# A fused attention and two-layer-stack kernel on one core: weight preparation timed by its own load, a swapped load buffer, a later restart of the conversion, one second product moved

## The chip, the cores and the metric

The kernel runs on one core of a Trainium2 chip. The metric is the device time of one execution in microseconds (us). "PE" is TensorE, "DVE" VectorE, "ACT" ScalarE, "POOL" GpSimd and "SP" SyncE, which here only issues DMAs.

## The reference, cut to what matters

```python
x = attention(q, k, v, mem_k, mem_v)          # windows of 32 queries, 56 keys with 8 memory keys; [1536, 512]
p = probs / (probs.sum(-1) + 1e-9)
y = sum(p[:, e] * (relu(x @ w1[e]) @ w2[e]) for e in range(4))     # w1[e]: 512 x 1024, w2[e]: 1024 x 512
h = y @ w_in                                   # 512 x 2048
out = (relu(h) + alpha * minimum(h, 0)) @ w_out                    # 2048 x 512
```

Everything is float32, but `w_in` and `w_out` reach the chip as 64-bit words and are turned into float32 there.

## The kernel before, in words

**The tiles.** After the attention the work is a row of 24 *pairs* of 128 hidden features: pairs 0 to 15 belong to the four experts, pairs 16 to 23 to the last layer. The two halves of the 1536 tokens are worked together, so a tile is a pair times 384 columns, and each pair has two tiles (columns 0 and 384). For a tile k there are two pieces of PE work. `gemm1` (line 565), the first product, is a Strassen-like scheme of seven products named by their banks in the order a, b, d, a, c, d, c, of 6 matmuls each, 42 in all. `gemm2` (line 652), the second product, has 8 blocks of 6 matmuls, all called `y`, 48 in all. Every matmul is 128x128 by 128x384. The 6 come from float32 split into a high and a low half: high by high, high by low, low by high.

**What the other engines do for a tile.** In `gemm1` ACT copies the first bank (`u`), DVE adds the banks (`u`, `t`, `b`, `d`, `c`), and bank a, d and c are each written a second time, which waits until those reads are done. `gelu` (line 593) makes the activation `g`: for the experts one DVE operation, for the last layer two on ACT and one on DVE. ACT casts it to the high half (`gg`) and POOL subtracts to get the low half. In `gemm2` each of the 8 blocks is added to `acc` by DVE (copied by ACT for pair 0, by DVE for pair 16).

**Order of the PE's work.** `order` (lines 758 to 769) is written out. It starts first product of tile 0, second of 0, first of 1, second of 1, then first of 2, first of 3, second of 2, and so on with the second product one tile behind. Pairs 14 and 15, and 16 and 17, are interleaved column by column (tiles 28 to 35); there two first products are followed by one double second product (`gemm2_two`, line 707, 96 matmuls). `acc` is the output of the experts there, and `transition` (line 183) turns it, one half of the columns at a time, into the next layer's input `xh`/`xl` with ACT, DVE and POOL, while tiles 30 and 31, then 32 and 33, are computed.

**The planner.** Each engine runs its program in the order in which it was written out. That order is made by a planner with a clock `now[0]`, which goes on by 0.013 + 384/2400 = 0.173 us with each matmul. Before each matmul it writes out whatever other work is due. There are two streams: "w" prepares the weights, "c" converts.

**Weights ("w", lines 375 to 468).** Each pair has a first matrix (z = 0) and a second (z = 1), 512 KB each. `load_raw` issues its DMA from SP into a buffer called raw0 or raw1, one of each. `prep_w1` makes four sums (`s`), then casts (ACT, `wh`) and subtracts (`wl`) seven pieces; `prep_w2` casts and subtracts two pieces of double size. Sums and subtractions are on POOL, for the pairs in `QUICK` = (1, 15, 17) on DVE at shorter steps (`DT_FAST` 0.45 instead of 1.1). At its end `prep_w1(p)` loads the next pair's first matrix, and `prep_w2(p)` the next second one. `WIDE` = (15, 17) are the pairs which need four extra pieces in tiles shared with the conversion (tags `ft`, `fr`), free only while `change[0]` is set and no conversion chunk is under way (`room_w1`). `weights` (line 460) gives the order: before a wide pair, its `prep_w1` comes ahead of the `prep_w2` of the pair before it. So `prep_w1(15)` and `prep_w1(17)` begin the moment after they issued their own loads.

**Conversion ("c", lines 473 to 514).** 32 chunks, four to a pair of the last layer, each a load (`fr`), five DVE operations (`fm`, `fw`), one on ACT, two on POOL (`fl`), and a store to `w2s` in DRAM, from where `load_raw` reads pairs 16 to 23. The planner starts one each 15 us (`T_CONV`), the DVE part 6 us behind the load. The first comes 20 us after tile 2's first product begins. None starts while `change[0]` is set, which is so from the first product of tile 27 to the beginning of that of tile 35.

Of the kernel before, what the change touches and what calls it, by code (L numbers as in the profile page):

```python
# [10 lines left out]
F32 = mybir.dt.float32  # L11
# [20 lines left out]
P = 128  # L32
# [4 lines left out]
NCOL = NT // 2  # L37
NP1 = E * F1 // (2 * P)
NP2 = F2 // (2 * P)
NP = NP1 + NP2  # L40
# [25 lines left out]
def tile_kernel(ctx: ExitStack, tc: tile.TileContext, qk, v, wa, wq, dpt, alpha, out):  # L66
# [6 lines left out]
    bp = ctx.enter_context(tc.tile_pool(name="bp", bufs=1))  # L73
# [29 lines left out]
    now = [0.0]  # L103
# [38 lines left out]
    change = [False]  # L142
# [226 lines left out]
                x[0] = now[0]  # L369

    w2s = dp.tile([NP2, P, 2048], F32, name="w2s")
    raws, w1, w2 = {}, {}, {}
    used1, used2 = set(), set()

    def load_raw(p, z):
        raw = bp.tile([P, 4, 256], F32, tag=f"raw{z}", name=f"raw{z}_{p}")
        src = wa[p] if p < NP1 else w2s[p - NP1]
        sync.dma_start(raw.rearrange("p a f -> p (a f)"), src[:, z * 1024:(z + 1) * 1024])
        raws[p, z] = raw

    ring1 = []

# [13 lines left out]
        ring1.append((p, j))  # L396
        return tuple(bp.tile([P, 256], F32R, tag=f"w1{x}", bufs=SLOTS, name=f"w{x}1_{p}_{j}") for x in "hl")

    def pace(p):
        fast = p in QUICK  # L400
        return dve if fast else pool, DT_FAST if fast else DT if p else DT_0

    loaded = [0.0]

    def pause(t, cond=None):
        return now[0] + t, cond

    def prep_w1(p):

        e, dt = pace(p)  # L410
        yield pause(0.0, lambda: (p, 0) in raws)
        raw = raws[p, 0]
        a11, a12, a22, a21 = (raw[:, i] for i in range(4))
        s = bp.tile([P, 4, 256], F32, tag="S", name=f"s_{p}")
        src = {A11: a11, A12: a12, A22: a22, S1: s[:, 0], S2: s[:, 1], S3: s[:, 2], S4: s[:, 3]}
        for zo, x, y, op in (
            (S1, a21, a22, ALU.add), (S2, s[:, 0], a11, ALU.subtract),
            (S3, a11, a21, ALU.subtract), (S4, a12, s[:, 1], ALU.subtract),
        ):
            e.tensor_tensor(out=src[zo], in0=x, in1=y, op=op)  # L420
            yield pause(dt)
        for j, z in enumerate(USE):
            yield pause(0.0, lambda: room_w1(p, j))
            h, l = place_w1(p, j)
            act.copy(h, src[z])
            yield pause(dt)
            e.tensor_tensor(out=l, in0=src[z], in1=h.bitcast(F32), op=ALU.subtract)
            w1[p, z] = (h, l)
            yield pause(dt)
        raws.pop((p, 0))  # L430
        if p + 1 < NP:
            yield pause(0.0, lambda: conv_done(p + 1))
            load_raw(p + 1, 0)
            loaded[0] = now[0]

    def prep_w2(p):

        e, dt = pace(p)
        yield pause(0.0, lambda: p < 2 or p - 2 in used2)
        if p == 1:  # L440
            yield pause(0.0, lambda: att["done"] == 2 * NU)
        if p == 0:
            yield pause(0.0, lambda: (0, 1) in raws and began)
        raw = raws.pop((p, 1))
        h = bp.tile([P, 4, 256], F32R, tag="w2", bufs=4, name=f"wh2_{p}")
        l = bp.tile([P, 4, 256], F32R, tag="w2", bufs=4, name=f"wl2_{p}")
        for z in (0, 2):
            act.copy(h[:, z:z + 2], raw[:, z:z + 2])
            yield pause(1.5 * dt)
            e.tensor_tensor(  # L450
                out=l[:, z:z + 2], in0=raw[:, z:z + 2], in1=h[:, z:z + 2].bitcast(F32), op=ALU.subtract
            )
            if z == 2:
                w2[p] = (h, l)
            yield pause(1.5 * dt)
        if p + 1 < NP:
            load_raw(p + 1, 1)
            yield pause(max(0.0, loaded[0] + 6.0 - now[0]))

    def weights():  # L460
        for p in range(NP):
            if p not in WIDE:
                yield from prep_w1(p)
            if p + 1 in WIDE:
                yield from prep_w1(p + 1)
            yield from prep_w2(p)

# [184 lines left out]
    def gemm2(p, c0, n, gs, soon, last):  # L652
        prep_force("w", lambda: p in w2)
        wh, wl = w2[p]
        y = {}

        def part(o, ab, i, start, stop, z0=0, z1=n):
            lag_poll(lambda: 2 * i + ab in gs)
            gh, gl = gs[2 * i + ab]
            if start:  # L660
                y[o, ab] = bank(f"y{p}_{c0}_{o}_{ab}_{z0}")[:, :n]
            w_ = [x[:, 2 * i + o // 2, (o % 2) * P:(o % 2 + 1) * P] for x in (wh, wl)]
            for k, (a, b) in enumerate(((w_[0], gh), (w_[1], gh), (w_[0], gl))):
                product(y[o, ab][:, z0:z1], a, b[:, z0:z1], n=z1 - z0,
                        start=start and k == 0, stop=stop and k == 2)
            if stop:
                evac(p, c0 + z0, z1 - z0, o, ab, y[o, ab][:, z0:z1])

        if p == 0:

            for o in range(2):
                part(o, 0, 0, True, False)
            for o in range(4):
                part(o, 1, 1, True, False)
                part(o, 1, 0, False, True)
            for o in range(2):
                part(o, 0, 1, False, True)
            for o in range(2, 4):
                part(o, 0, 0, True, False)
                part(o, 0, 1, False, True)  # L680
        elif soon:

            for o in range(4):
                part(o, 0, 0, True, False)
            for o in range(2):
                part(o, 1, 1, True, False)
            for o in range(4):
                part(o, 0, 1, False, True)
            for o in range(2):
                part(o, 1, 0, False, True)  # L690
        else:
            for o in range(4):
                part(o, 0, 0, True, False)
                part(o, 0, 1, False, True)
            for o in range(2):
                part(o, 1, 1, True, False)
                part(o, 1, 0, False, True)
        for o in range(2, 4) if p else ():

            end = p == NP - 1 and c0 + n == NCOL and o == 3  # L700
            for z0, z1 in ((0, n // 2), (n // 2, n)) if end else ((0, n),):
                part(o, 1, 1, True, False, z0, z1)
                part(o, 1, 0, False, True, z0, z1)
        if last:
            used2.add(p)
# [49 lines left out]
    k0 = len(FIRST)  # L755
    kc = tiles.index((NP1 - 2, 0, half))
    order = []
    for k in range(k0):
        order += [(1, k), (2, k)]
    order += [(1, k0)]  # L760
    for k in range(k0 + 1, kc + 1):
        order += [(1, k), (2, k - 1)]
    order += [(1, kc + 1), (2, kc, kc + 1)]
    for k in range(kc + 2, kc + 8, 2):
# [21 lines left out]
    for i, (what, k, *other) in enumerate(order):  # L786
        p, c0, n = tiles[k]
        if k == k0 and what == 1:
            dve.tensor_scalar_mul(nalpha, nalpha, -1.0)
        if what == 1:  # L790
            if p == 0:
                while att["done"] < 4 * -(-(c0 + n) // BLK):
                    if k == 0:
                        att_cycle()
                    else:
                        att_poll(force=True)
                    prep_poll()
                    while begun and att["next"] >= begun[0][0]:
                        begun.pop(0)[1]()
                    if att["done"] >= 3 and not gated:  # L800
                        gated.append(gate())
                        begun.append((11, lambda: load_pb(0, *FIRST[0])))
                        begun.append((12, lambda: load_raw(0, 1)))
            if k == k0 - 1:
                attention_over()
            if k == k0:
                stream("c", convert())
                streams["c"][0] = now[0] + 20.0
            if k + 1 < len(tiles):
                p1, d0, m = tiles[k + 1]  # L810
                if p1 < NP1 and (2 * p1 * P // F1, d0, m) not in pb_t:
                    load_pb(2 * p1 * P // F1, d0, m)
            if p >= NP1 and f"x{c0}" in streams:
                prep_force(f"x{c0}", lambda: f"x{c0}" not in streams)
            began.append(k)
            change[0] = kc - 1 <= k < kc + 7
            acts[k] = gemm1(p, c0, n, k % 2 if p else 0, k == final[p])
        else:
            if other:
                gemm2_two(p, c0, n, [acts.pop(k), acts.pop(k + 1)], k == final[p])  # L820
            else:
                gemm2(p, c0, n, acts.pop(k), order[i - 1] == (1, k), k == final[p])
            if p == NP1 - 2:
                stream(f"x{c0}", transition(c0, n))
# [19 lines left out]
DT_FAST = 0.45  # L844
DT_CONV = 1.2
T_CONV = 15.0
DT_X = 1.1
RING = 4
RINGV = 3
# [75 lines left out]
```

## Time and profile before

| | |
|---|---|
| median of 3 runs | 852.46 us (851.75 to 853.57) |
| the profiled execution | 852.93 us, span 851.2 us |
| PE busy | 824.9 us of the span, 97% |
| DVE, ACT, POOL busy | 583.2, 336.9, 552.9 us |
| mean granted clock of PE | 0.99 of full speed |

Times in the rows below are from the start of the span. The profiled execution is 0.47 us above the median. A row of the timeline gives start, duration, engine, line and operation, with its output and inputs; in brackets stands how long the engine sat idle before it and what ended that.

### The profile page before, as it was taken

Reading aid. Unit: us, or ns where it says so; the run is one execution under the profiler, and the core shown is the slowest. Engines: PE = TensorE matmul, PEld = TensorE weight load, DVE = VectorE, ACT = ScalarE, POOL = GpSimd, SP = SyncE. Lnnn points to the kernel's source line nnn. Section 1 sums busy time; section 2 is a strip of 40 time slices with the busy share of each in tenths; the row PEclk is TensorE's granted clock in tenths of the full one; section 3 lists DMA queues with packets and bytes.
Section 4 is the critical chain, followed back from the end, with each engine's and each line's share of the span. In section 5 each row is a group of like instructions: output and inputs, shape, how many; then the busy total and the mean of one; then the engine's idle time right before and its main releaser. Section 6 shows DMA issues by size and latency. Waiting matters only on the chain.

```text
span 851.2 us, 15052 instructions
## 1 busy us (share of the span) xinstructions
PE 824.9 (97%) x5659; PEld 799.2 (94%) x5659; DVE 583.2 (69%) x1157; ACT 336.9 (40%) x754; POOL 552.9 (65%) x584
## 2 busy tenths in 40 slices
PE   8888999999999999999999999998898999999998
PEld 6656999999999999999999999998897999999998
DVE  4768656876777777776877857368844767666555
ACT  2555642232332332322322332145652746546432
POOL 3548466777877877867877944283743887876611
PEclk9999999999999999999999999999998999999999
DMA  8784202323312332322332212001002222221003
GB/s 234 191 245 140 75 10 78 97 89 100 112 52 86 124 105 80 99 85 77 106 106 75 87 38 75 1 26 50 25 17 71 87 79 89 82 75 50 1 1 148
DMA packets 30600, 71.70 MB, mean 84 GB/s; under 512 B 4800, under 2 KB 11072, under 8 KB 30528
## 3 DMA queue, kind: packets, MB, share of 16 engines
q1 hardware_dynamic: 30528, 70.75, 26.2%
q8 instruction: 44, 0.72, 0.4%
q14 instruction: 28, 0.23, 0.1%
HBM read 59.18 MB, written 11.56 MB: 83 GB/s over the span
## 4 chain that ended last, share of the span: by engine, by line
PE 83%; DVE 5%; POOL 4%; DMA 4%; issue 2%; ACT 2%; SPq 1%; DVEq 0%; POOLq 0%; ACTq 0%
PE y L60 43%; PE a L60 10%; PE c L60 10%; PE d L60 10%; PE b L60 5%; POOL gg L60 2%; POOL xl L60 1%; DMA v<-in_v 1%; POOL wl L60 1%; PE keep L60 1%; PE x L60 1%; DVE acc L60 1%; DVE s L60 1%; DMA raw<-w2s 1%; PE two L60 1%
## 5 line engine op out<-in xcount | busy, mean ns | idle before, releaser
L60 PE MATMUL y<-gg,wh 128*128 128x384 f32 x1540 | 403.6, 339 | 4.1 <-POOL gg L60 2.2
L60 PEld LDWEIGHTS y<-gg,wh 128*128 128x128 f32 x1540 | 280.4, 189 | 6.7 <-POOL gg L60 4.1
L60 POOL TENSOR_TENSOR gg<-g,gg 128x384 fp32r<-128x384 f32 x192 | 199.9, 1051 | 126.0 <-ACT gg L60 100.4
L60 PE MATMUL y<-gg,wl 128*128 128x384 f32 (+1 forms) x770 | 260.0, 338 | 0.0
L60 DVE TENSOR_TENSOR acc<-y,acc 128x384 f32<-128x384 f32 x321 | 171.4, 551 | 63.3 <-PE y L60 62.1
L60 ACT CAST gg<-g 128x384 fp32r<-128x384 f32 x192 | 97.5, 512 | 169.0 <-DVE g L60 168.9
L60 POOL TENSOR_TENSOR wl<-raw,wh 128x256 fp32r<-128x256 f32 (+1 forms) x105 | 105.2, 1014 | 77.3 <-ACT wh L60 49.3
L60 PEld LDWEIGHTS y<-gg,wl 128*128 128x128 f32 x770 | 145.4, 189 | 0.0
L60 ACT COPY u<-a 128x384 f32<-128x384 f32 x48 | 23.0, 479 | 179.5 <-PE a L60 179.5
L60 POOL TENSOR_TENSOR wl<-s,wh 128x256 fp32r<-128x256 f32 x84 | 65.3, 786 | 8.2 <-ACT wh L60 6.6
L60 PE MATMUL a<-xh,wh 128*128 128x384 f32 x184 | 62.7, 341 | 2.6 <-ACT u L60 2.6
L60 ACT CAST wh<-raw 128x256 fp32r<-128x256 f32 (+1 forms) x116 | 55.0, 493 | 24.9 <-DMA raw<-in_wa 11.9
L60 DVE TENSOR_TENSOR u<-b,u 128x384 f32<-128x384 f32 x48 | 26.7, 556 | 54.1 <-PE b L60 45.6
L60 PE MATMUL d<-xh,wh 128*128 128x384 f32 x184 | 62.5, 340 | 1.0 <-DVE t L60 1.0
L60 PE MATMUL a<-xl,wh 128*128 128x384 f32 x184 | 62.3, 339 | 0.0
L60 PE MATMUL a<-xh,wl 128*128 128x384 f32 x184 | 62.3, 338 | 0.0
L60 PE MATMUL d<-xl,wh 128*128 128x384 f32 x184 | 62.0, 337 | 0.0
L60 PE MATMUL d<-xh,wl 128*128 128x384 f32 x184 | 62.0, 337 | 0.0
L60 PE MATMUL c<-xh,wh 128*128 128x384 f32 x176 | 60.0, 341 | 0.0
L60 PE MATMUL c<-xh,wl 128*128 128x384 f32 x176 | 59.9, 341 | 0.0
L60 PE MATMUL c<-xl,wh 128*128 128x384 f32 x176 | 59.6, 339 | 0.0
L60 POOL TENSOR_TENSOR fl<-fl,fm 128x512 f32<-128x512 f32 x32 | 41.5, 1296 | 25.5 <-DVE fm L60 11.4
(113 smaller groups left out, 1398.6 us busy)
## 6 DMA issues: line engine op xcount, KB each, us to landing
raw<-in_wa SPq DMA_DIRECT2D x32, 512.0 KB, 3.7
fr<-in_wq SPq DMA_DIRECT2D x32, 512.0 KB, 3.9
w2s<-fl SPq DMA_DIRECT2D x32, 256.0 KB, 2.4
raw<-w2s SPq DMA_DIRECT2D x16, 512.0 KB, 3.6
qk<-in_qk SPq DMA_DIRECT2D x24, 312.0 KB, 4.8
v<-in_v SPq DMA_DIRECT2D x32, 130.0 KB, 4.5
pb<-p_dram SPq DMA_DIRECT2D x8, 384.0 KB, 3.5
outT<-acc SPq DMA_DIRECT2D x15, 192.0 KB, 1.9
```

The costliest lines, as they stand in the source:

```text
L60: return self.tc.keep_in_program_order(f(*a, **kw))
```

## The change: what it does

- The second product of tile 1 (pair 0, columns 384) moves behind the first product of tile 2. Its blocks run in the usual order, and its activations use the other set of buffers.
- `prep_w1` and `prep_w2` (but for the first pairs) wait until the planner's clock is 7 us (9 us for pairs 15 and 17) past the issue of their load; the pause of 6 us behind a load goes.
- `prep_w1(15)` comes behind `prep_w2(14)` instead of ahead of it. `prep_w1(17)` still comes ahead of `prep_w2(16)`.
- `prep_w2(16)` subtracts on DVE instead of POOL.
- Pair 17's second matrix is loaded into raw0, as soon as `prep_w1(17)` is through with it; pair 18's first matrix goes into raw1 after `prep_w2(16)`. From there on the two buffers have changed places.
- `change[0]` is set until tile 35's first product is over: the conversion resumes one first product later.

```diff
-    raws, w1, w2 = {}, {}, {}
+    raws, landed, w1, w2 = {}, {}, {}, {}
...
-        raw = bp.tile([P, 4, 256], F32, tag=f"raw{z}", name=f"raw{z}_{p}")
+        raw = bp.tile([P, 4, 256], F32, tag=f"raw{z if p + z < NP1 + 2 else 1 - z}", name=f"raw{z}_{p}")
...
+        landed[p, z] = now[0] + T_LOAD[p in WIDE]
...
-    def pace(p):
-        fast = p in QUICK
+    def pace(fast, p):
...
-        e, dt = pace(p)
-        yield pause(0.0, lambda: (p, 0) in raws)
+        e, dt = pace(p in QUICK, p)
+        yield pause(0.0, lambda: (p, 0) in raws and (p == 0 or landed[p, 0] <= now[0]))
...
-        if p + 1 < NP:
+        if p == NP1 + 1:
+            load_raw(p, 1)
+        elif p + 1 < NP:
             yield pause(0.0, lambda: conv_done(p + 1))
             load_raw(p + 1, 0)
-            loaded[0] = now[0]
...
-        e, dt = pace(p)
+        e, dt = pace(p in QUICK or p == NP1, p)
         yield pause(0.0, lambda: p < 2 or p - 2 in used2)
+        if p > 1:
+            yield pause(max(0.0, landed[p, 1] - now[0]))
...
-        if p + 1 < NP:
+        if p == NP1:
+            load_raw(p + 2, 0)
+        elif p + 1 < NP:
             load_raw(p + 1, 1)
-            yield pause(max(0.0, loaded[0] + 6.0 - now[0]))
...
-            if p not in WIDE:
+            if p != NP1 + 1:
                 yield from prep_w1(p)
-            if p + 1 in WIDE:
+            if p == NP1:
                 yield from prep_w1(p + 1)
...
-        if p == 0:
+        tight = p == 0 and c0 + n < NCOL
+        if tight:
...
-        for o in range(2, 4) if p else ():
+        for o in () if tight else range(2, 4):
...
-    for k in range(k0):
+    for k in range(k0 - 1):
         order += [(1, k), (2, k)]
-    order += [(1, k0)]
-    for k in range(k0 + 1, kc + 1):
+    order += [(1, k0 - 1)]
+    for k in range(k0, kc + 1):
         order += [(1, k), (2, k - 1)]
...
-            change[0] = kc - 1 <= k < kc + 7
-            acts[k] = gemm1(p, c0, n, k % 2 if p else 0, k == final[p])
+            change[0] = kc - 1 <= k < kc + 8
+            acts[k] = gemm1(p, c0, n, k % 2, k == final[p])
         else:
+            change[0] = change[0] and k < kc + 6
...
+T_LOAD = (7.0, 9.0)
```

Here NP1 = 16 is the first pair of the last layer, k0 = 2, kc = 28.

## Rows read from the trace of the kernel before

**Rows 1.** The page: busy times; a group's count, busy us, mean ns, idle before it:
```profile
PE 824.9 (97%) x5659; PEld 799.2 (94%) x5659; DVE 583.2 (69%) x1157; ACT 336.9 (40%) x754; POOL 552.9 (65%) x584
...
L60 DVE TENSOR_TENSOR acc<-y,acc 128x384 f32<-128x384 f32 x321 | 171.4, 551 | 63.3 <-PE y L60 62.1
```

**Rows 2.** The chain that ended last: start, length, what (with count):
```profile
467.49 8.42 PE y L60 x48
483.20 8.37 PE y L60 x48
...
516.19 8.39 PE y L60 x48
...
531.92 16.80 PE y L60 x96
...
604.15 16.82 PE y L60 x96
...
635.82 3.71 DMA fr<-in_wq
...
659.49 1.04 PE a L60 x6
...
674.27 8.36 PE y L60 x48
```

**Rows 3.** Windows of 5 us: PE, PEld, DVE, ACT, POOL busy; PEclk, DMA share, GB/s:
```profile
585.00:590.00 5.00, 3.89 (x13) 3.89 (x14) 3.42 (x8) 3.45 (x7) 4.14 (x4) 0.66 0.15 56
...
645.00:650.00 5.00, 4.05 (x13) 3.89 (x13) 1.32 (x3) 0.00 (x0) 4.54 (x4) 0.50 0.63 213
```

**Rows 4.** Timeline of PE: first matmuls of tile 1's second product and of tile 2:
```profile
97.16 0.33 PE L60 MATMUL y<-gg,wh 128*128 128x384 f32 x1
...
106.88 0.34 PE L60 MATMUL a<-xh,wh 128*128 128x384 f32 x1
```

**Rows 5.** Timeline of DVE where pair 15's first matrix is prepared:
```profile
506.72 0.43 DVE L60 TENSOR_TENSOR s<-raw 128x256 f32<-128x256 f32 x1 [4.11 <-DMA raw<-in_wa]
```

**Rows 6.** Timelines of DVE, ACT and PE around tile 32's first product:
```profile
573.84 0.42 DVE L60 TENSOR_TENSOR s<-raw 128x256 f32<-128x256 f32 x1 [5.20 <-DMA raw<-w2s]
...
585.06 0.62 ACT L60 CAST xh<-acc 128x512 fp32r<-128x512 f32 x1 [1.53 <-DVE acc L60]
...
586.11 0.45 PE L60 MATMUL a<-xh,wh 128*128 128x384 f32 x1 [2.61 <-ACT u L60]
...
591.96 0.34 PE L60 MATMUL a<-xh,wh 128*128 128x384 f32 x1
```

**Rows 7.** Timelines of ACT, DVE and PE in tile 33's first product:
```profile
590.62 0.50 ACT L60 ACTIVATE g<-b 128x384 f32<-128x384 f32 x1 [1.44 <-DVE b L60]
...
593.26 0.62 ACT L60 CAST wh<-raw 128x512 fp32r<-128x512 f32 x1 [1.09 <-DMA raw<-w2s]
...
596.77 0.47 ACT L60 COPY u<-a 128x384 f32<-128x384 f32 x1
...
597.29 0.45 PE L60 MATMUL a<-xh,w 128*128 128x384 f32 x1 [2.05 <-ACT u L60]
...
598.44 0.68 DVE L60 TENSOR_TENSOR wl<-raw,wh 128x512 fp32r<-128x512 f32 x1
...
600.79 0.45 PE L60 MATMUL d<-xh,w 128*128 128x384 f32 x1 [1.12 <-DVE t L60]
...
601.34 0.96 DVE L60 TENSOR_TENSOR st<-acc 128x256 f32<-128x256 f32 x1
...
602.84 0.44 PE L60 MATMUL c<-xh,w 128*128 128x384 f32 x1 [0.73 <-DVE b L60]
```

**Rows 8.** Timeline of DVE where the conversion resumes:
```profile
639.56 0.43 DVE L60 TENSOR_SCALAR fm<-fr 128x512 uint32<-128x512 uint32 x1 [4.81 <-DMA fr<-in_wq]
```

**Rows 9.** Timeline of SP: the last store of converted weights, pair 23's loads:
```profile
762.28 0.32 SPq L511 DMA_DIRECT2D w2s<-fl  x1
...
775.47 5.16 SPq L60 DMA_DIRECT2D raw<-w2s  x2
```

More of the change, by code (lines that the diff above doesn't have):

```diff
@@ L397, in place_w1 @@
         return tuple(bp.tile([P, 256], F32R, tag=f"w1{x}", bufs=SLOTS, name=f"w{x}1_{p}_{j}") for x in "hl")
-    def pace(p):
-        fast = p in QUICK
+    def pace(fast, p):
         return dve if fast else pool, DT_FAST if fast else DT if p else DT_0
-    loaded = [0.0]
     def pause(t, cond=None):
```

## The prediction

> **What bounds the kernel now.** I read the page's first part, then the chain that ended last, then windows over its gaps, then the timelines of single engines there. PE is busy 97% of the span [rows 1], so nothing is won by making another engine faster; what can be won is time in which PE waits or runs slowly. The chain shows where that is. From one second product to the next takes 483.20 − 467.49 = 15.71 us in the undisturbed stretch: 8.4 of second product, 7.3 of first product, 0.174 us for each of the 90 matmuls [rows 2]. Against that, around the change from the experts to the last layer:
>
> - 483.20 to 516.19 is two such tiles, 31.4 us of work in 33.0: **1.6 lost**, in tile 28.
> - 531.92 + 16.80 = 548.72 is the start of tile 30's first product. Two of 7.3 and a double second product of 16.8 put tile 32's first product at 580.1. Tile 33 begins at 591.96 [rows 6] instead of 587.4: **4.55 lost**. The double second product follows at 604.15 instead of 599.3: **4.9 lost**.
> - That one ends at 620.97. With two first products and a double second product the next part is due at 652.4 and comes at 659.49: **7.1 lost**. From there to 674.27 two first products take 14.8, with 0.2 lost.
>
> In all 18.35 us. Outside this stretch there is one more place that the change touches: tile 1's second product takes 106.88 − 97.16 = 9.72 us for 8.4 of work [rows 4], **1.3 lost**.
>
> **The change part by part.**
>
> *The moved second product.* It began at once behind its own first product and waited for activations (POOL's low halves). With tile 2's first product between, 7.3 us cover them, and the 1.3 go. Tile 2's weights and inputs must then be there 9.7 us earlier; they are prepared during tile 1's first product and PE showed no wait for them. What is late next is DVE: its adds and activations for tile 1, mostly written out at the end of that first product, now stand right ahead of tile 2's adds. That may give back 0 to 0.6; I take 0.3. Gain **1.0**. Nothing else on the path: no instruction is added. Since the conversion's clock starts with tile 2's first product, all its chunks also come 8.3 planner us earlier, so one more fits before the break (by the planner's arithmetic the 25th missed it by 0.3 us), and 7 are left behind it.
>
> *Pair 15.* `prep_w1(15)` was written out right behind its load, so DVE stood 4.11 us for the DMA [rows 5] with the evacuations of a second product and tile 28's adds behind it; PE then waited for `t`. Now POOL's `prep_w2(14)` comes first and DVE's part 9 us behind the load, and a DMA of that size takes 3.7 [rows 2]. In the 9.3 us into which the sums and subtractions now fall DVE has 11 of them at 0.43 [rows 5] and some 12 adds, activations and evacuations at 0.55 [rows 1], 11.3 us; overlapped ends make it less, so it may fall behind by 1 or 2 us, less than the slack of eight banks at 1.05 us. Gain 1.6, taken as **1.5**.
>
> *Pair 17's first matrix.* The same with 5.20 us of DVE waiting from 568.64 to 573.84 [rows 6]. The evacuations piled up, ACT's cast of `acc` waited for the last of them until 585.06, the copy `u` stands behind it on ACT, and PE sat 2.61 us for `u`. Then the clock was granted at 0.66 over the 5 us window, its lower level of 1.2 GHz for part of it [rows 3], with matmuls 0.32 us apart. The load landed just ahead of 573.84; DVE's program now has the sums 9 us of matmuls further on, which makes it 577, or 576 if DVE was 1 us behind the matmuls there. So 2 to 3 us are spare, DVE evacuates on time, and all **4.5** go.
>
> *Pair 17's second matrix, and 16's on DVE.* In tile 33 ACT waited 1.09 us for that DMA [rows 7], and `u` came 2.05 us late. With the load into raw0 the cast comes 9 us later and finds its data. But ACT was full there: from `g<-b` at 590.62 to the end of `u` at 597.24 are 6.6 us with only 1.09 of waiting, and it keeps a cast of that size (0.62) in between, now pair 16's second. So PE still waits for `u`, 2.05 − 1.09 = 1.0 us. The wait for `t` (1.12) loses DVE's subtraction ahead of it (598.44, 0.6 to 0.68 us) and keeps 0.5; the wait for `b` (0.73) is kept. That leaves 2.2, and 0.3 for pair 17's second matrix, which is now ready only as the double second product reaches it: 2.5 of the 4.9 stay, gain **2.4**. The bounds are 0 (ACT and DVE, with 7 casts and 11 subtractions of pair 17 moved towards this stretch and two operations moved from POOL, fall behind as far as the DMA made them) and 4.9.
>
> Row and rule differ here. The sums `st` of the same shape as the 0.42 us ones took up to 0.96 in this tile while POOL was at work [rows 7]; POOL's four sums for pair 18 were part of that and now come later, so the waits could also be shorter than I take. The Trainium skill, page SBUF — State Buffer, section Who interferes with whom, says that a DVE instruction with two SBUF inputs and a GpSimd one reading SBUF exclude each other, and the one behind waits for the whole other. By that rule moving pair 16's two subtractions to DVE is no gift: each could stand behind a whole POOL operation, and 1.5 to 2 us would be added to the 2.5 left.
>
> *The conversion's restart.* `fr` shares a buffer with the last piece of pair 17's first matrix, so its load could only go out when PE was through with it, at 635.82 [rows 2], while DVE's first conversion step was written out ahead of tile 35's last adds: 4.81 us of waiting [rows 8]. `gg` came late, PE waited four times in 5 us, and the clock fell to 0.50 for the window 645 to 650 [rows 3], 1.2 GHz. Now load and step stand a first product later; the load goes out at the same place of PE's work, the step 6 us behind it for 3.7 of DMA. All 7.1, taken as **7.0**.
>
> *What costs nothing.* Elsewhere the wait of 7 us behind a load equals the 6.9 us that the second matrix's four steps of 1.65 took. SP's order changes only there: pair 17's second ahead of pair 18's first. Pair 18's first matrix arrives 10 us later than before, but its pieces need slots that tile 34 frees. The last store stood 13 us ahead of pair 23's load [rows 9]; with one chunk less behind the break (16 us each) and 7 us less of PE work the margin grows to some 20 us.
>
> Sum: 1.0 + 1.5 + 4.5 + 2.4 + 7.0 = 16.4. Against the profiled execution's 852.93 (span 851.2 and 1.7 around it) that is 836.5; the median is 0.47 lower, so I forecast 836.2.
>
> **The rivals.**
>
> *All of it goes.* With POOL less busy and DVE on time tile 33 runs without waits: 2.4 becomes 4.9, and the roundings 0.5 more: 833.3. For it: half of the waits are for DVE operations stretched by POOL. Against: ACT's own chain of 6.6 − 1.09 = 5.5 us is longer than the 5.2 us (five products of 1.04) after which PE wants `u`.
>
> *ACT and DVE become the bound in tiles 32 and 33.* The casts and subtractions of pair 17 and pair 16's second matrix now fall into these 15 us, some 36 DVE operations of 0.43 to 0.68 us, up to 20 us if none overlap. Tile 33 keeps 4.9, up to 1 more in the double second product, and if the idle time reaches the 2.61 of tile 32, the clock falls again for 1.6 us: 836.2 + 2.4 + 1 + 1.6 = 841.2. By the SBUF page's rule in the Trainium skill it would be some 838, within this span; the 0.96 us of rows 7 agrees with it.
>
> *The load is still late.* POOL issues pair 17's load at the end of its own backlog; if that grows by over 3 us, DVE waits again and up to 4.5 come back: 840.7.
>
> *Slower.* The conversion ends too late. Should the extra chunk not fit before the break and the restart cost more than the 7 us, pair 23's weights come behind their use. It decides only from three chunks (48 us) later than I reckon, where the margin of 20 and the 10 us of preparation slack are gone and some 18 us of PE waiting replace the 16.4: about 854.5. For it speaks that the margin was only 13 us before; against it that the change adds to it.
>
> **How the numbers follow.** Forecast 0.62, all of it 0.15, ACT and DVE 0.14, load late 0.04; together faster 0.95. That the stalls only move and the sum is nothing 0.02; slower 0.03. A measurement tells about 0.2% from no change, 1.7 us. The range 833.0 to 841.5 takes in the bounds of tile 33's term and the first three rivals.
>
> **What would show it.** No DVE wait for a `raw` or `fr` DMA between 500 and 650; double second products 31.4 us apart, but for about 2.5 us more in tile 33, with PE waiting there for `u`, `t` and `b`; granted clock 1.00 from 550 to 650; tile 1's second product in 8.4 us. A DVE idle of some us ended by a raw DMA, a second low-clock window, or a PE wait for `wl` in pairs 17, 18 or 23 would prove me wrong.

## The result, and the profile after the change

The changed kernel takes **841.13 us** (median of 4 runs, 839.44 to 842.48) against 852.11 for the kernel before on the same chip: a ratio of 0.9872, 95% interval 0.9844 to 0.9899. A second time, on another chip, it was 841.57 (6 runs) and 0.9885 (0.9863 to 0.9907). The forecast was 836.2 with 833.0 to 841.5 as its range: the direction was right, and the time came out 4.9 us above the forecast, 0.4 below the upper end of the range. The second median is 0.1 above that end.

PE does the same work in a shorter span (page of the kernel after, engines' busy time):

```profile
PE 818.6 (97%) x5659; PEld 794.0 (95%) x5659; DVE 588.3 (70%) x1159; ACT 337.0 (40%) x754; POOL 557.0 (66%) x582
```

The chain of waits shows where the time went, by the starts of the second products. Of the kernel after, start, duration, what:

```profile
306.87 8.36 PE y L60 x48
...
315.68 5.77 DMA fr<-in_wq
...
324.61 8.43 PE y L60 x48
...
482.13 8.37 PE y L60 x48
...
513.75 8.39 PE y L60 x48
529.46 16.79 PE y L60 x96
...
630.58 16.82 PE y L60 x96
```

Read against [rows 2]: from 482.13 to 513.75 are 31.6 us for two tiles, so pair 15's loss is gone. But 306.87 to 324.61 are 17.7 instead of 15.7, with a load of `fr` in the chain: **a loss that the kernel before did not have**. I cut both timelines of PE at the same places, the first matmuls of products (us; the work alone is 7.3 for a first and 8.4 for a second product):

| stretch | before | after | after, second profile |
|---|---|---|---|
| up to the first product of tile 1 (attention) | 89.87 | 87.51 | 85.62 |
| to tile 2's second product | 31.58 | 30.76 | 30.76 |
| to tile 14's second | 188.78 | 188.44 | 188.44 |
| to tile 15's second | 15.76 | 17.73 | 17.39 |
| to tile 26's second | 172.70 | 173.19 | 173.15 |
| to tile 27's second | 17.34 | 15.96 | 15.97 |
| to tile 32's first | 64.15 | 64.14 | 64.13 |
| tiles 32 and 33, first products | 23.81 | 20.13 | 20.15 |
| their double second product | 16.82 | 17.74 | 17.73 |
| tiles 34 and 35, with their double second product | 38.52 | 31.64 | 31.63 |
| the next two first and two second products, and one first | 38.79 | 39.40 | 39.44 |
| to the last second product | 132.91 | 133.05 | 132.91 |
| sum without the first line | 741.16 | 732.18 | 731.70 |

Behind the attention part two profiles of one kernel agree within 0.35 us per stretch, mostly 0.02. The attention part differed by 4.3 us over the 14 profiles of this study (85.62 to 89.87); it is what makes single times scatter. So the stretches judge the parts of the change, and the medians the whole.

The waits that are left, in PE's timeline of the kernel after (start, us, operation, in brackets the idle time ahead and what ended it):

```profile
98.35 0.44 PE L60 MATMUL a<-xh,wh 128*128 128x384 f32 x1 [0.27 <-ACT u L60]
...
583.66 0.44 PE L60 MATMUL d<-xh,wh 128*128 128x384 f32 x1 [0.57 <-DVE t L60]
585.41 0.44 PE L60 MATMUL c<-xh,wh 128*128 128x384 f32 x1 [0.43 <-DVE b L60]
590.92 0.45 PE L60 MATMUL a<-xh,w 128*128 128x384 f32 x1 [1.08 <-ACT u L60]
594.14 0.44 PE L60 MATMUL d<-xh,w 128*128 128x384 f32 x1 [0.84 <-DVE t L60]
596.71 0.44 PE L60 MATMUL c<-xh,w 128*128 128x384 f32 x1 [1.24 <-DVE b L60]
...
603.92 0.44 PE L60 MATMUL y<-gg,wl 128*128 128x384 f32 x1 [0.47 <-DVE wl L60]
```

They answer to [rows 6, 7]. By the first matmuls of products tile 32 takes 8.83 us instead of 11.78 (1.5 lost, 4.5 before), tile 33 11.31 instead of 12.03 (4.0 lost, 4.7 before). The clock, which fell to its lower level in [rows 3], stays at 1.00 (windows; columns: stretch, busy us of PE, PEld, DVE, ACT, POOL, granted clock, DMA share, GB/s):

```profile
585.00:590.00 5.00, 4.43 (x24) 4.11 (x24) 3.74 (x8) 4.46 (x10) 1.99 (x2) 1.00 0.32 114
645.00:650.00 5.00, 5.00 (x30) 5.00 (x29) 1.52 (x3) 1.62 (x3) 1.73 (x2) 1.00 0.14 52
```

DVE's timeline: its waits of 4.11 and 5.20 us for a `raw` load [rows 5, 6] are gone, and one of 2.55 for `fr` is new. The last four rows, from tile 33, stand beside two rows of POOL's timeline, below them:

```profile
321.54 0.43 DVE L60 TENSOR_SCALAR fm<-fr 128x512 uint32<-128x512 uint32 x1 [2.55 <-DMA fr<-in_wq]
...
511.04 0.41 DVE L60 TENSOR_TENSOR s<-raw 128x256 f32<-128x256 f32 x1
...
574.21 0.42 DVE L60 TENSOR_TENSOR s<-raw 128x256 f32<-128x256 f32 x1
...
592.53 1.08 DVE L60 TENSOR_TENSOR st<-acc 128x256 f32<-128x256 f32 x1
593.54 0.55 DVE L60 TENSOR_TENSOR t<-d,u 128x384 f32<-128x384 f32 x1
594.00 0.75 DVE L60 TENSOR_TENSOR st<-acc,st 128x256 f32<-128x256 f32 x1
594.68 1.50 DVE L60 TENSOR_TENSOR st<-acc 128x256 f32<-128x256 f32 x1
```

```profile
592.31 2.16 POOL L60 TENSOR_TENSOR gg<-g,gg 128x384 fp32r<-128x384 f32 x2 [2.27 <-PE a L60]
594.43 2.33 POOL L60 TENSOR_TENSOR xl<-acc,xh 128x512 fp32r<-128x512 f32 x2
```

A sum of that shape takes 0.41 us alone. Here the three `st` take 3.33 instead of 1.23, and `t` and `b`, for which PE waits, stand behind them on DVE.

### The profile page after: what moved, and what is told of

Same layout as the page of the kernel before. It is cut to its first block, busy times and chain, and to the rows that moved or that the text cites. A ratio compares the mean times of both kernels' runs of the same rounds, so it can differ in the third digit from the quotient of the medians.

```text
span 839.8 us, 15057 instructions
## 1 busy us (share of the span) xinstructions
PE 818.6 (97%) x5659; PEld 794.0 (95%) x5659; DVE 588.3 (70%) x1159; ACT 337.0 (40%) x754; POOL 557.0 (66%) x582
## 4 chain that ended last, share of the span: by engine, by line
PE 87%; DVE 4%; DMA 3%; ACT 2%; POOL 1%; issue 1%; SPq 1%; DVEq 0%; ACTq 0%; POOLq 0%
PE y L60 47%; PE a L60 11%; PE c L60 11%; PE d L60 10%; PE b L60 5%; DMA v<-in_v 2%; PE keep L60 1%; PE x L60 1%; SPq L60 1%; ACT g L60 1%; DMA fr<-in_wq 1%; DVE g L60 1%; PE xt L60 1%; DMA qk<-in_qk 1%; DVE wl L60 1%
## 5 line engine op out<-in xcount | busy, mean ns | idle before, releaser
L60 POOL TENSOR_TENSOR gg<-g,gg 128x384 fp32r<-128x384 f32 x192 | 202.6, 1065 | 138.3 <-ACT gg L60 117.1
L60 DVE TENSOR_TENSOR u<-b,u 128x384 f32<-128x384 f32 x48 | 26.7, 556 | 56.0 <-PE b L60 53.8
L60 ACT CAST wh<-raw 128x256 fp32r<-128x256 f32 (+1 forms) x116 | 54.3, 491 | 15.2 <-PE y L60 14.6
```

Of the source, the lines that this page charges most:

```text
L60: return self.tc.keep_in_program_order(f(*a, **kw))
```

## The experiments

**The new stall, and the moved product.** Two kernels tell whether the move of tile 1's second product causes the stall at 322 us, and how. One undoes the move, the other keeps it and sets back only the conversion's clock, which starts with tile 2's first product.

```diff
 # e1_no_move
-        tight = p == 0 and c0 + n < NCOL
+        tight = p == 0
...
-    for k in range(k0 - 1):
+    for k in range(k0):
...
-            acts[k] = gemm1(p, c0, n, k % 2, k == final[p])
+            acts[k] = gemm1(p, c0, n, k % 2 if p else 0, k == final[p])
 # e2_conv_phase
-                streams["c"][0] = now[0] + 20.0
+                streams["c"][0] = now[0] + 28.3
```

Expected of the first: 

> Kernel after with one part undone: the second product of tile 1 stands right behind its own first product again. The conversion's clock then starts where it did in the kernel before, and by the planner's arithmetic its chunks fall on the same tiles as before. Theory (the move gains about 1.0 us at tile 1, and loses some 2 us later because every chunk falls 8.3 planner us earlier against the tiles): the 2 us that PE loses at 320 to 325 us, with DVE standing over 2 us for the load of fr, are gone, tile 1's second product takes 9.7 us again, and the total is some 840 to 841, 0 to 1.5 below the 841.1 of after. Rival (the stall at 322 us has another cause, such as the new order of the raw loads): it stays, and the total is some 842 to 843.

Expected of the second: 

> Kernel after with the conversion's clock started 8.3 planner us later, so that its chunks stand on the planner's clock where the kernel before had them, while tile 1's second product stays moved. Theory (phase of the chunks): no wait of DVE for fr over 0.5 us up to 480 us, second products 15.7 us apart at 306 to 325 us instead of 17.7, total 838.5 to 839.5. Rival (the move itself or the order of loads causes the stall): 17.7 us there again and 841 in total. One chunk more is left behind the break than in after (8 instead of 7); with last stores 16 us apart it should still lie ahead of pair 23's load and cost nothing; if not, pair 23's weights come late and the total rises by several us.

Measured: 842.83 us (ratio 0.9901, 0.988 to 0.9922) and 842.00 (0.9893, 0.9877 to 0.9908). Neither total is below that of the kernel after, as the theory wanted; with intervals of 0.3 to 0.4% totals cannot tell 2 us here (the attention part was 88.87 us in the profile of e2_conv_phase, 87.51 in that of the kernel after). The stretches do: to tile 15's second product 15.77 and 15.76 us in both, against 17.73 and 17.39; to tile 26's 172.70 in both, against 173.2. Every other profile with the conversion's clock at its place of before (c1, c2, c3 and c5 below) has 15.76 there too, every one without 17.35 to 17.76. Behind the attention e2_conv_phase sums to 730.15, 1.6 and 2.0 less than the two profiles of the kernel after: 0.4 of what it wins in these stretches it loses ahead of them (188.84 up to tile 14's second product, against 188.44). Undoing the move brings tile 2's second product back to 31.58 us. In e1_no_move tile 33 also takes 11.89 us instead of 11.31. Its three waits there are those of the kernel after (1.09, 0.83 and 1.26 us), but here the clock fell behind them, to 1.2 GHz for part of a window:

```profile
595.00:600.00 5.00, 5.00 (x21) 5.00 (x21) 2.37 (x6) 4.50 (x10) 2.02 (x2) 0.66 0.00 0
```

How the phase makes a stall is seen on SP's queue. First the kernel after, then e2_conv_phase (start, us to issue, transfer):

```profile
312.62 0.33 SPq L60 DMA_DIRECT2D raw<-in_wa  x1
315.25 0.32 SPq L513 DMA_DIRECT2D w2s<-fl  x1
315.68 0.37 SPq L488 DMA_DIRECT2D fr<-in_wq  x1
317.77 0.33 SPq L60 DMA_DIRECT2D raw<-in_wa  x1
```

```profile
313.24 2.84 SPq L60 DMA_DIRECT2D raw<-in_wa  x2
319.18 0.33 SPq L488 DMA_DIRECT2D fr<-in_wq  x1
322.96 0.33 SPq L513 DMA_DIRECT2D w2s<-fl  x1
```

In e2_conv_phase the next chunk's `fr` goes out at 319.18, as the last reader of the buffer ends (`fw<-fr,fm` at 318.47, 0.68 us), and the store of the chunk before follows. In the kernel after that reader ended at 309.86, but the load went out at 315.68 (DVE's and POOL's timelines):

```profile
309.18 0.68 DVE L60 SCALAR_TENSOR_TENSOR fw<-fr,fm 128x512 uint32<-128x512 uint32 x1
...
313.93 1.30 POOL L60 TENSOR_TENSOR fl<-fw,fl 128x512 f32<-128x512 f32 x1
```

Of these 5.8 us SP stood 2.8 at a `raw` load, which it issued at 312.62. Only the 2.7 behind that were spent at the store, which waited for POOL's `fl` until 315.23. The transfer of `fr` then took 5.77 us, against 3.8 in e2_conv_phase. The 2.7 alone are enough for DVE's wait of 2.55. SP's list of instructions shows why: in both kernels each load stands ahead of the store of the chunk before it, up to the break; in the kernel after one pair stands the other way round, this one, among the `raw` loads of pair 9. That the phase makes the stall is shown; that it does so by the order of this one pair is read from the queue and was not tried alone.

**The conversion's restart.** It resumes one first product sooner again, as in the kernel before:

```diff
-            change[0] = kc - 1 <= k < kc + 8
+            change[0] = kc - 1 <= k < kc + 7
```

> Kernel after with one part undone: the conversion resumes one first product earlier, as in the kernel before. Theory (fr's buffer is the last piece of pair 17's first matrix, so the load waits for PE and the step written out ahead of it for the load): DVE stands 4 to 5 us for fr at about 625 us, the double second product behind it comes about 7 us later, with a granted clock near 0.5 in some 5 us, total 847 to 849. Rival (in the kernel before the step was only late because the tiles ahead of it were late): the wait for fr is below 2 us and the total 841 to 843.

Measured: 847.75 us (ratio 0.9964, 0.9954 to 0.9973). Tiles 34 and 35 with their double second product take 38.78 us instead of 31.64, and the wait and the low clock are back (DVE's timeline, and a window):

```profile
634.80 0.43 DVE L60 TENSOR_SCALAR fm<-fr 128x512 uint32<-128x512 uint32 x1 [4.73 <-DMA fr<-in_wq]
```

```profile
640.00:645.00 5.00, 3.89 (x13) 3.65 (x12) 1.56 (x3) 0.00 (x0) 4.78 (x5) 0.56 0.61 207
```

The theory holds: the tiles ahead of this place are as in the kernel after (37.88 us for tiles 32 and 33 and their double second product, against 37.87), and the loss is back all the same. The stretch behind it takes 38.87 instead of 39.40: the later restart gives 0.5 back there.

**The wait behind pair 17's first load, and its other buffer.** Each undone alone:

```diff
 # e8_w17_now
-        landed[p, z] = now[0] + T_LOAD[p in WIDE]
+        landed[p, z] = now[0] + (0.0 if p == NP1 + 1 and z == 0 else T_LOAD[p in WIDE])
 # e7_raw1
-        raw = bp.tile([P, 4, 256], F32, tag=f"raw{z if p + z < NP1 + 2 else 1 - z}", name=f"raw{z}_{p}")
+        raw = bp.tile([P, 4, 256], F32, tag=f"raw{z}", name=f"raw{z}_{p}")
...
-        if p == NP1 + 1:
-            load_raw(p, 1)
-        elif p + 1 < NP:
+        if p + 1 < NP:
...
-        if p == NP1:
-            load_raw(p + 2, 0)
-        elif p + 1 < NP:
+        if p + 1 < NP:
```

> Kernel after with one part undone: no wait behind the load of pair 17's first matrix. By the planner's arithmetic its sums, casts and subtractions are then written out 9 us sooner, ahead of the evacuations of the double second product, and pair 16's and 17's second matrices 5 to 9 us sooner. Theory (the wait removes DVE's stall for the transfer, and pays for part of that by moving 11 DVE operations and 7 casts into tile 32 and more into tile 33): DVE stands 4 to 5 us for the transfer, tile 32 takes 10.5 to 12 us, but tile 33 only 9 to 10.5 instead of 11.3, together 1 to 3 us more than after. Rival (both terms stand by themselves): tile 32 as long as in before, 11.9, tile 33 as in after, 11.3, 3 us more in total.

Measured: 843.40 us (one run). DVE stands for the transfer again and PE for `u` (DVE's and PE's timelines):

```profile
572.11 0.43 DVE L60 TENSOR_TENSOR s<-raw 128x256 f32<-128x256 f32 x1 [5.43 <-DMA raw<-w2s]
```

```profile
584.38 0.44 PE L60 MATMUL a<-xh,wh 128*128 128x384 f32 x1 [2.66 <-ACT u L60]
```

Tile 32 takes 11.98 us (3.15 more; the granted clock is 0.80 from 582 to 587 us and 0.86 from 587 to 592), but tile 33 10.43 and the double second product 16.82 (0.9 less each). So the wait is worth 1.4 us, not 4.5: it takes DVE's stall away and pays with work moved into tile 33.

> Kernel after with one part undone: pair 17's second matrix is loaded into raw1 again, behind the preparation of pair 16's second, and pair 18's first goes ahead of it. By the planner's arithmetic pair 17's second matrix is then cast 2.8 us later. Theory (with the fixed wait behind the load ACT no longer stands for that transfer, so the buffer only sets when the matrix is ready): tile 33 takes 11.3 us as in after, within 0.5, and the double second product behind it waits some 3 us for the low half wl instead of 0.5, so 2 to 3 us more in total. Rival (the other buffer is what saved tile 33's time): tile 33 itself is 1 us or more longer, with ACT standing for the transfer.

Measured: 846.17 us (one run). Tiles 32 and 33 take 20.14 us, as in the kernel after, so the theory's half holds; the double second product takes 23.18, 5.4 more and not 3 (PE's timeline, and a window of five us around the end of the second wait):

```profile
603.43 0.45 PE L60 MATMUL y<-gg,wh 128*128 128x384 f32 x1 [0.97 <-ACT wh L60]
606.27 0.69 PE L60 MATMUL y<-gg,wl 128*128 128x384 f32 x1 [2.40 <-DVE wl L60]
```

```profile
605.00:610.00 5.00, 3.73 (x12) 3.73 (x13) 3.94 (x5) 0.62 (x1) 4.79 (x5) 0.50 0.32 105
```

PE waited 3.4 us for the two halves of the weights and the clock stood at 0.50, 1.2 GHz: 12 matmuls in 3.73 us, against 30 in 5.00. Of the 6.4 us above the work alone 3.4 are these waits, and the lower clock makes up most of the rest.

**What fills tiles 32 and 33.** Besides the weights, the transition (the last layer's inputs: casts `xh`, sums `st`, differences `xl`) of the second half runs there. One kernel leaves it out; one moves it later; two more also bring pair 17's weights sooner, and one of them moves the transition further; the last brings only the weights sooner. All but the first two also have e2_conv_phase's edit.

```diff
 # e9_x_none
     def transition(c0, n):
+        if c0:
+            return
 # e5_x_late
     def transition(c0, n):
+        if c0:
+            yield now[0] + X_WAIT, None
...
-                yield now[0] + DT_X, None
+                yield now[0] + (DT_XL if c0 else DT_X), None
...
+X_WAIT = 10.0
+DT_XL = 0.8
 # c1_x10_w17: the same X_WAIT and DT_XL; c2_x14_w17: 14.0 and 0.6; c3_w17: neither
-        landed[p, z] = now[0] + T_LOAD[p in WIDE]
+        landed[p, z] = now[0] + ((9.0, 6.3)[z] if p == NP1 + 1 else T_LOAD[p in WIDE])
 # (7.5, 7.8) in c2_x14_w17 and c3_w17
```

> Kernel after without the preparation of the second half's inputs for the last layer: the casts, sums and differences of columns 384 to 767 of the last layer's input are left out, so these columns are multiplied as they stood in the layer before. All else is as in after. Theory (in tiles 32 and 33 these operations of DVE, ACT and POOL, and DVE's sums stretched from 0.41 to as much as 1.5 us beside POOL, make the products wait): tile 32 takes at most 8.0 us instead of 8.8, tile 33 at most 9.3 instead of 11.3, and no DVE sum or difference there is stretched by over 0.2 us. Rival (the weights of pairs 16 and 17 and the chain from g to u on ACT are what is too much): tile 33 stays above 10.5.

> Kernel after with the second half's casts, subtractions and sums of the last layer's input (wh, wl and st made on ACT, DVE and POOL beside tiles 32 and 33) begun 10 planner us later and taken 0.8 instead of 1.1 apart, so that fewer of them share tiles 32 and 33 with pair 17's and pair 16's preparation. Theory (ACT, DVE and POOL are too full in tiles 32 and 33): tile 33 comes 15.7 us minus 8.4, so 7.3 to 8, behind tile 32 and the double second product 7.3 to 9 behind tile 33, instead of 8.8 and 11.3; 3 to 5 us less in total, 836 to 838. Rival (ACT's own chain from g to u sets it, whatever else is prepared): tile 33 keeps 11, total 840 to 841. Third way (the operations are only moved): what is won in tile 32 and 33 is lost at tile 34, whose inputs then come late, total 841 or more.

> Kernel after with three edits: the conversion's clock 8.3 planner us later as in e2_conv_phase, the second half's transition 10 us later with steps of 0.8 as in e5_x_late, and pair 17's second matrix cast 6.3 instead of 9.0 planner us behind its load. Theory (the second half's transition costs 4.5 us in tiles 32 and 33 and their double second product; e5_x_late won 2.4 of it in the two tiles, and lost 1.3 behind them because wl came late): no stall of 2 us at 322, tiles 32 and 33 together 17.8 us or 0.5 more, the double second product 16.8 to 17.2 instead of 19.0; counted from the start of tile 1's first product to the last second product 727 to 728 instead of 732; total 836.5 to 838.5. Rival (the earlier casts of pair 17's second matrix only move the wait into tile 33): tiles 32 and 33 take 19 us, total 838.5 to 840.

> As c1_x10_w17, but the second half's transition 14 us later with steps of 0.6, and pair 17's first matrix 7.5 instead of 9.0 planner us behind its load (its second matrix then 7.8, so at the same place). Theory: tile 33 is freed of nearly all transition work, tiles 32 and 33 together 16 to 17.3 us, the double second product 16.8 to 17.2, total 0.5 to 1.5 us below c1_x10_w17. Rival (the transition then ends too late for tile 34): 1 to 3 us are lost in the first product behind the double second product, which took 14.8 for it and the next until now, and the total is equal to c1_x10_w17 or above.

> Kernel after with the conversion's clock as in e2_conv_phase and pair 17's matrices sooner as in c2_x14_w17, the second half's transition left where it is. Theory (what is too much is the sum of weights and transition in tiles 32 and 33, so moving weights by 1.5 to 2.7 us inside these tiles wins little): tiles 32 and 33 together 19.5 to 20.5 us (20.1 in after), the double second product 16.8 instead of 17.7, total 838 to 840. Rival (w2(17) late and pair 17's first matrix are the cost): both tiles together under 18.5 us, total 837 or less.

In the expectation of e5_x_late `wh` and `wl` stand for `xh` and `xl`. Measured (the stretches of the table above; work alone 14.6 and 16.8):

| kernel | tiles 32 and 33 | double second product | both | total us (ratio, interval) |
|---|---|---|---|---|
| after | 20.13 | 17.74 | 37.87 | 841.57 (0.9885, 0.9863 to 0.9907) |
| e9_x_none | 16.07 | 17.31 | 33.38 | 837.62 (one run) |
| e5_x_late | 17.77 | 19.00 | 36.77 | 843.04 (0.9901, 0.9883 to 0.9919) |
| c1_x10_w17 | 17.79 | 20.68 | 38.47 | 840.17 (0.9869, 0.9849 to 0.9889) |
| c2_x14_w17 | 14.86 | 21.94 | 36.80 | 838.83 (0.9857, 0.9835 to 0.9879) |
| c3_w17 | 19.91 | 17.08 | 36.99 | 839.10 (0.9868, 0.9841 to 0.9896) |

Without the transition PE's timeline has two waits left in both tiles, and no `st` to be stretched (one difference `wl` still took 0.96 beside a `gg` of POOL, against my 0.2):

```profile
585.10 0.45 PE L60 MATMUL c<-xh,wh 128*128 128x384 f32 x1 [0.38 <-DVE b L60]
590.10 0.45 PE L60 MATMUL a<-xh,w 128*128 128x384 f32 x1 [0.49 <-ACT u L60]
```

So the second half's transition costs 4.5 us of the 6.5 lost. But moving it won only 1.1, because the wait moves with it. The totals of e5_x_late (836 to 838 expected) and c1_x10_w17 (836.5 to 838.5) were missed. c2_x14_w17 lies 1.3 below c1_x10_w17, as expected, but with a double second product 4.7 us longer than I gave it. It runs both tiles without a wait of PE and then stands in the double second product; c1_x10_w17, for which I expected at most 17.2 there, waits 0.29 and 1.49 us for `gg` at the same place, and the clock falls to 0.78 in the window behind. PE's timeline, POOL's and a window of c2_x14_w17:

```profile
599.43 0.61 PE L60 MATMUL y<-gg,wh 128*128 128x384 f32 x2 [3.09 <-POOL gg L60]
```

```profile
594.44 0.74 POOL L60 TENSOR_TENSOR s<-raw 128x256 f32<-128x256 f32 x1
595.14 1.29 POOL L60 TENSOR_TENSOR xl<-acc,xh 128x512 fp32r<-128x512 f32 x1
596.39 1.17 POOL L60 TENSOR_TENSOR s<-s,raw 128x256 f32<-128x256 f32 x1
597.52 0.90 POOL L60 TENSOR_TENSOR xl<-acc,xh 128x256 fp32r<-128x256 f32 x1
598.39 2.41 POOL L60 TENSOR_TENSOR gg<-g,gg 128x384 fp32r<-128x384 f32 x2
```

```profile
600.00:605.00 5.00, 5.00 (x22) 5.00 (x21) 4.97 (x8) 0.62 (x1) 5.00 (x5) 0.66 0.00 0
```

Four POOL operations stand ahead of the last `gg` on its queue, and the clock falls for part of the window behind the wait. My rival for this kernel, tile 34 late, did not come (31.64). c3_w17 came out as expected: sooner weights alone win 0.9.

**A version that is faster than both.** c2_x14_w17 with POOL's `xl` of the second half made by DVE: two instructions less ahead of `gg`, and fewer of POOL's beside DVE's.

```diff
-        e = dve if fast else pool
+        e, el = dve if fast else pool, dve if fast == 2 else pool
...
-        pool.tensor_tensor(out=xl[:, 0:4, cs], in0=acc[:, :, 0, cs], in1=xh[:, 0:4, cs].bitcast(F32), op=sub)
+        el.tensor_tensor(out=xl[:, 0:4, cs], in0=acc[:, :, 0, cs], in1=xh[:, 0:4, cs].bitcast(F32), op=sub)
...
-                pool.tensor_tensor(out=xl[:, 4:6, cs], in0=b22, in1=xh[:, 4:6, cs].bitcast(F32), op=sub)
+                el.tensor_tensor(out=xl[:, 4:6, cs], in0=b22, in1=xh[:, 4:6, cs].bitcast(F32), op=sub)
...
-            for _ in prep_x(d0, BLK, True):
+            for _ in prep_x(d0, BLK, 2 if c0 else 1):
```

> Kernel c2_x14_w17 with one edit: the low halves xl of the second half that POOL made, two in each of three blocks, are made by DVE. c2_x14_w17 ran tiles 32 and 33 in 14.9 us with no loss, but its double second product took 21.9 instead of 16.8: POOL had two of those xl (1.29 and 0.90 us) and two sums for pair 18 ahead of the last activations gg, PE waited 3.09 us for gg, and ran at the lower clock in part of the 5 us behind. Theory (POOL's queue ahead of gg, and DVE and POOL slowing each other, DVE's sums and differences taking up to 1.69 us beside POOL's): gg comes 2 us sooner, PE waits under 1.2 us for it, the clock stays at 1.00, the double second product takes 17 to 18.5 us, tiles 32 and 33 still 14.9 to 15.4, total 834 to 836. Rival (DVE is full by itself there, with six more operations of 0.4 to 0.7 us): gg waits for DVE instead of POOL, or tile 34's first product for the last xl, and the total is 838 or more.

Measured: **835.49 us** (5 runs, 834.87 to 836.63), a ratio of 0.9817 (0.979 to 0.9845), below the whole interval of the kernel after in its second measurement; with that of c2_x14_w17 its interval overlaps, and there the stretches tell. Tiles 32 and 33 take 14.85 us, the double second product 19.01: 33.86 in all, 2.9 less than in c2_x14_w17. PE's wait and POOL's queue ahead of it:

```profile
599.29 0.62 PE L60 MATMUL y<-gg,wh 128*128 128x384 f32 x2 [1.69 <-POOL gg L60]
```

```profile
596.22 0.74 POOL L60 TENSOR_TENSOR s<-raw 128x256 f32<-128x256 f32 x1
597.04 0.80 POOL L60 TENSOR_TENSOR s<-s,raw 128x256 f32<-128x256 f32 x1
597.80 2.60 POOL L60 TENSOR_TENSOR gg<-g,gg 128x384 fp32r<-128x384 f32 x2
```

The wait is 1.69 where I had under 1.2: two sums for pair 18 still stand ahead, and the two `gg` take 2.60 instead of 1.99 beside DVE's differences. The clock stays at 1.00, where it was 0.66 in c2_x14_w17. Six operations more on DVE, which was the fuller engine (in c2_x14_w17 8.50 us busy from 590 to 600, POOL 7.56), made the stretch shorter. POOL's shorter queue and its sharing with DVE were changed together, so no run divides the 2.9 us between them.

## Why the prediction was right in its sign and 4.9 us off

- **The moved second product**: forecast 1.0, measured 0.82 (31.58 to 30.76). What failed is the sentence "Nothing else on the path". I saw that all chunks come 8.3 planner us earlier and asked only how many fit ahead of the break (right: one more, 7 left). Their new phase against the tiles costs 2.0 us in one tile and 0.5 in those behind it, 1.6 to 2.0 in all after the 0.4 that it saves ahead. A shift of a whole stream should have been a rival of its own.
- **Pair 15**: forecast 1.5, measured 1.38 in its stretch, where DVE's wait for the load is gone. Right, though no run undid this part alone.
- **Pair 17's first matrix**: the DMA wait went as forecast, and the load had time to spare (issued at 568.22, 3.6 us long, used at 574.21). "All 4.5 go" failed: 2.95 went. The sum put at nothing what the wait moves into tiles 32 and 33, and e8_w17_now shows that, net of this, the wait is worth 1.4.
- **Pair 17's second matrix, and 16's on DVE**: forecast 2.5 left, measured 4.0 in tile 33 and 0.9 in the double second product. Of the gain of 2.4 nothing came: tile 33 is 0.7 shorter, the double second product 0.9 longer. (The prediction's 4.9 lost in tile 33 sets a start from the chain against one from PE's timeline, 0.16 us apart; from PE's timeline alone it is 4.7.) The wait for `u` was sized rightly (1.0 forecast, 1.08), the chain on ACT too. Those for `t` and `b` were not (0.84 and 1.24 for 0.5 and 0.73). I counted which operations are left ahead of them, at their durations of before; the transition's `st` now fell beside POOL's `gg` and `xl` and took 2.1 us more than alone. Also, the brackets add up to 3.16 of the 4.0: counted by the starts of PE's matmuls, each of the three stops costs 0.27 us more than its bracket. No run set pair 16's two subtractions back to POOL, so what they gave or cost stays open.
- **DVE and POOL side by side**: `st`, with both inputs in SBUF, took up to 1.50 us instead of 0.41, 1.09 more, about one POOL operation, while `t`, with one input in PSUM, took its usual 0.55 beside the same `gg`. The Trainium skill, page SBUF — State Buffer, section Who interferes with whom, says that a DVE instruction with two SBUF inputs and a GpSimd one that reads SBUF exclude each other. The trace agrees with it. In the prediction this rule was worth 1.5 to 2 us and was set aside. The stretched `st` account for the direction and at most for the 0.85 us by which the waits for `t` and `b` were longer than I took; of the 2.4 us missing in tile 33 and behind it, 0.84 are the 0.27 at each stop, and 0.65 the late `wl`. c5_xl_dve does not test it, because POOL's queue became shorter at the same time.
- **The conversion's restart**: forecast 7.0, measured 6.88, by the cause named (e3_resume_early). Of this it lost 0.6 in the tiles behind.
- **The rivals**: "ACT and DVE become the bound" gave 841.2 and came nearest, but by a sum of other parts: tile 33 kept 4.0 of its 4.7 and the double second product lost 0.9 as it said, the clock did not fall, and tile 32's 1.5 and the stall at 322 us were not in it. It also named the weights alone: without the transition, 4.5 us go with the weights left in place, and what leaving out weights would give was not run. The two rivals with a late load or a late conversion did not come: the load had 2.5 us to spare, and the last store went out at 737.49, 26.7 us ahead of pair 23's first load. Of the signs against the prediction one came, a small one: PE waited 0.47 us for pair 17's `wl` in the double second product, for which 0.3 had been set down.
- **The sum**: 1.0 + 1.5 + 4.5 + 2.4 + 7.0 = 16.4 became 0.82 + 1.38 + 2.76 + 6.88 = 11.84, of which 2.9 were given back elsewhere (2.0 at 322 us; 0.5, 0.6 and 0.1 in other stretches; 0.3 was won ahead of it). That is 8.98 behind the attention. The other 2.4 of the 11.3 between the two profiles are the attention part, where one profile of before does not tell chance from effect; by the medians the gain is 10.4 to 11.0. The granted clock differed there too: over the first 85 us it was 0.96 in the profile of before, 0.98 and 1.00 in the two of the kernel after. Whether a part of the 2.4 is the change's stays open. (The last step of the prediction's sum, 852.93 − 16.4 − 0.47, is 836.1 and not 836.2.)
- **What was luck**: the sum was 4.6 us too large in its terms, and 2.9 were lost outside them, 7.4 in all. In these two profiles the attention part, which the prediction does not name, gave 2.4 of it back. That the time still lies within the range is owed to this and to bounds wide enough for the rivals, not to the sum.

## What to carry to other kernels

When a stall is removed by moving work, list what runs on every engine in the stretch that receives it, and price it by durations measured beside the same neighbours: here one stretch of three products held weights, transition and activations, and five arrangements of it ended within 1.7 us of each other. What helped was to shorten the queue of the engine for which PE stood, by giving POOL's subtractions to DVE, although DVE was the fuller engine. And a background stream that starts from an event moves as a whole when that event moves, so look at every transfer order that its new phase can change.

## What the runs showed of the hardware that I had not expected

- Two profiles of one kernel agree to 0.35 us per stretch behind the attention, mostly to 0.02, while the attention part ahead of it scattered by 4.3 us over 14 profiles. Parts of this change could be told from single profiles to some tenths of a us where medians of four to six runs could not tell 2 us.
- PE's waits of 2.40, 2.66 and 3.09 us (e7_raw1, e8_w17_now, c2_x14_w17) ended in or just ahead of windows at a granted clock of 0.50 to 0.86, and so did two of 0.29 and 1.49 within 2 us (c1_x10_w17, 0.78), while 1.92 alone (e5_x_late) and 1.69 alone (c5_xl_dve) did not. The same three waits of 0.8 to 1.3 within 6 us were followed by a window of 0.66 in tile 33 of e1_no_move and by 1.00 in tile 33 of the kernel after. So the lengths of the waits alone do not tell it.
- A store that waited for its data on SP's queue held back the load behind it by 2.7 us although that load's buffer was free, and a load ahead of both had held it back by 2.8 before.
